# Free order of the four row tiles for matmul chains in a kernel whose order is planned

## The chip, the cores and the metric

The kernel runs on one core of a Trainium2 chip. A core has five engines that work from queues of their own: TensorE (PE), which does matmuls, VectorE (DVE), ScalarE (ACT), GpSimd (POOL), and SyncE (SP), whose queue here only starts DMA transfers. The metric is the device time of one execution in microseconds. In this kernel TensorE is used in three ways: with the whole 128x128 array ("whole" matmuls), as four row tiles of 32 rows that each take matmuls of their own ("row" matmuls, 32x128 in the profile), and as four column tiles of 32 columns (128x32 in the profile, for the weighted values of the attention).

## The reference

A row of x (2048 rows of 448 elements) is layer-normed to xn; then attention and a gated feed-forward both read xn, and their results are added to x. The attention has 16 query heads of 28 elements and one key and one value head. The numbers are float32.

```python
q = (x @ wq).reshape(B, S, H, Dh) ...; k = x @ wk; v = x @ wv
p = softmax(einsum("bhqd,bkd->bhqk", q, k) * Dh ** -0.5)
attention = einsum("bhqk,bkd->bhqd", p, v) ... @ wo
gate, up = xn @ w1, xn @ w3
feed_forward = (silu(gate) * up) @ w2
return x + attention(xn) + feed_forward(xn)
```

## The kernel before

**Precision.** Most matmuls run on operands in a reduced type (fp32r). An operand is split into a high part and the rest, and a product is the sum of high x high, high x rest and rest x high. So each product is a chain of many matmuls that add into one bank of PSUM, of which there are eight.

**Stages.** The 2048 rows are four blocks of 512 columns (`NQ`, `TC`). In the beginning all blocks are normed, transposed (xp) and projected to q, k and v (`project`, line 640: sixteen chains q, four for each block). The weights are loaded, split, used, and written to DRAM split for the later blocks. Then the attention goes in 16 groups of four heads (`NW`): for each head a first score tile gives a bound of the maximum (`leads`, ld), then 15 further score tiles (`product`, line 853, sc, three row matmuls each; head h uses row tile h mod 4), each followed by ScalarE's exponential (line 909). The weighted values (`values`, line 912, av) come in bursts of 6, 6 and 4 key tiles (`BURSTS`); a burst of 6 is 48 matmuls in the profile, one of 4 is 32. Beside the attention the feed-forward goes in 56 steps: gate and up (g, u, `gate_up`, line 754) for 128 hidden columns, and after two or three such steps four down projections (dn, `down`, line 775). The attention's output projection (wo, `out_project`, line 1021) and dn are added to acc, which is stored at the end of a block.

**Chains.** `chain` (line 443) builds q, g, u, dn and wo. With `first=None` it uses whole matmuls (11 for q, g and u). Otherwise every term of 128 rows becomes four row matmuls, one for each row tile: 42 for q, g and u. All matmuls of tile 0 come first, then those of tile 1, 2 and 3; each matmul depends on the one before. A bank may be written by one row tile at a time, so a chain that passes to the next tile waits until its last matmul in the former tile is done: `build` puts a `nop` with a dependency on that matmul in PE's queue. `WHOLE = (3, 2)` says that the first three steps of the feed-forward, and the query projections of the first two blocks, are whole; the last dn and wo are whole as well.

**The planner.** The order of all instructions on all queues is not that of the program text. Every operation is an `Op` with an engine, a modelled cost and latency, a priority (a due time from `due`, `begin` and others plus a correction `PUT` by kind of operation), and the operations it depends on. `Plan.order` (line 173) goes through time and gives each engine that is free its ready operation of the smallest key; for PE each of the four row tiles is a slot that is filled by itself (`SLOTS`). `BOOST` lowers the key of matmuls that continue a product or a chain. An operation is held back if its buffers are short (`MOST`, `SPARE`, `SOON`) or its PSUM bank is read by another engine (`locked`). If PE has nothing for a slot, a second pass takes operations before their time, if `EARLY` buffers are left. `FLIGHT = 4` is the largest number of chains of row matmuls that are begun and not ended: `link` is +1 at the first and -1 at the last matmul of a chain. Several chains may alternate in one tile. The queues of the chip then run in this order, each engine's instructions one after the other; where the model errs, an instruction waits at the head of its queue.

Of the kernel before, what the change touches and what calls it, by code (L numbers as in the profile page):

```python
# [38 lines left out]
ROWS = 4  # L39
BOOST = (97.61, 1.0)  # L40
FLIGHT = 4
WHOLE = (3, 2)
# [8 lines left out]
T0, TG, LEAD, SPAN = 59.41, 51.88, 5.12, 37.1  # L51
XDUE = (18.51, 11.88, 15.8, 24.23)
QDUE, QSTEP = 36.59, 9.52
SINGLE = 2
XSTORE = 13.37, 47.32
MDUE, MRUSH, MSTEP = 35.96, 8, 9.02
MEND = 12.77
# [4 lines left out]
BACKLOG = 1998.39  # L62
LATE = 765.84
HLV = 0
EARLY = 12
BULK = ("w13", "w2", "x", "raw", "raw2", "acc")
SOON = {"acc": 9.76, "h": 11.77, "mb": 12.24, "o": 44.69, "pa": 20.77, "pb": 55.73, "qs": 2, "w13": 109.34,
        "w2": 18.75, "wo": 69.88, "x": 31.37}

PUT = {"ACT ": 25.95, "ACT acc xn": 19.89, "ACT at pa": -2.13, "ACT at pb": 55.24, "ACT at x": -16.88,  # L70
# [3 lines left out]
        "DVE ": -6.21, "DVE acc": 11.86, "DVE acc mi": -6.67, "DVE acc xn": -7.18, "DVE at": 19.67,  # L74
# [8 lines left out]
        "POOL raw": 3.84, "POOL raw w13": -46.77, "POOL raw wo": 4.7, "POOL raw2 w2": 61.66,  # L83
# [12 lines left out]
SPARE = {"acc": 7, "h": 0, "qs": 5, "qt": 1, "raw": 4, "raw2": 1, "w13": 1, "w2": 2, "wo": 1, "x": 1}  # L96
# [23 lines left out]

class Op:
    __slots__ = ("eng", "cost", "lat", "fn", "bufs", "deps", "prio", "n", "wait", "outs", "at", "done", "size", "next", "k", "port", "row", "mode", "prev", "key", "link", "hop", "ins")


class Plan:
# [11 lines left out]
    def op(self, eng, cost, fn, reads=(), writes=(), parts=(), prio=0.0, after=(), lat=None, size=0, also=(), behind=None, k=16, port=False, row=None, mode="a", prev=None, nth=9):  # L137
# [18 lines left out]
        o.prio += PUT.get(eng + " " + " ".join(sorted({b.sort for b in o.bufs})), 0.0)  # L156
        for b in o.bufs:
            b.left += 1
        o.link, o.hop = 0, False
        if prev is not None and prev.row != row:  # L160
            prev.hop = True
        o.key = o.prio - (0.0 if prev is None else BOOST[0] if nth < 3 else BOOST[1])
        o.deps = list(deps.values())
        o.next = []
        for d in o.deps:
            (d.next if eng == d.eng in ("PE", "ACT", "POOL") and not (d is prev and d.row != row) else d.outs).append(o)
        if behind is not None:
            behind.next.append(o)
        o.wait = len(o.deps) + (behind is not None)
        self.ops.append(o)  # L170
        return o

    def order(self):
# [25 lines left out]
        def can(o, early=False):  # L199
# [9 lines left out]
            if early:  # L209
                if any(len(p) - k < EARLY for k, p in zip(need[:2], pools) if k):  # L210
                    return False
            elif any(o.prio > head() + SOON.get(sorts[c], 40.0) for c in cats):
                return False
# [17 lines left out]
        flying = 0  # L231
# [7 lines left out]
        while todo:  # L239
            progress = True  # L240
            while progress:
                progress = False
                for e, row in self.SLOTS:
# [3 lines left out]
                    for o in ready[e]:  # L247
                        if row is not None and (o.row not in (None, row) or o.link > 0 and flying >= FLIGHT):
                            continue
                        if best is not None and (o.key, o.n) >= (best.key, best.n):  # L250
                            continue
                        if e == "SP" and max(queues) - now > BACKLOG and o.prio > 40.0 and o.bufs and any(b.cat in BULK for b in o.bufs):
# [3 lines left out]
                        best = o  # L256
                    if best is None and e == "PE":
                        best = min((o for o in ready[e] if o.row in (None, row) and not (o.link > 0 and flying >= FLIGHT) and
                                    locked(o, now) <= now and can(o, True)),
                                   key=lambda o: (o.key, o.n), default=None)  # L260
# [28 lines left out]
                    if e == "PE":  # L289
# [6 lines left out]
                        flying += o.link  # L296
# [23 lines left out]
            while events and events[0][0] <= now + 1e-6:  # L320
                _, _, kind, o = heapq.heappop(events)
                if kind == "port":
                    continue
# [66 lines left out]
def build(ctx, tc, x, wqkv, w13r, wor, w2, out, flag):  # L390
# [52 lines left out]
    def chain(dst, n, w, width, terms, prio, after=(), whole=True, first=None):  # L443

        o = None
        whole = [d for l, _, r, _, _ in terms for d in l.writers + r.writers] if whole else []
        if first is None:
            todo = [(None, t) for t in terms]
        else:
            todo = [(r, t) for r in [(first + i) % ROWS for i in range(ROWS)] for t in terms if r in t[4]]  # L450
        for i, (r, (lb, lv, rb, rv, _)) in enumerate(todo):
            q = slice(0, P) if r is None else slice(r * RP, (r + 1) * RP)

            def fn(i=i, lb=lb, lv=lv, rb=rb, rv=rv, q=q):
                return nc.tensor.matmul(dst.ap[0:n, 0:width], lv(lb)[q], rv(rb)[q], start=(i == 0),  # L455
                                        stop=(i == len(todo) - 1))
            o = pe(width, fn, reads=[lb, rb], parts=[dst], prio=prio, row=r, prev=o,
                   after=[o] if o is not None else [*after, *whole])
            dst.writers = [o]
            if r is not None:  # L460
                o.link = (i == 0) - (i == len(todo) - 1)
# [605 lines left out]
    for o in todo:  # L1067
# [165 lines left out]
```

## Time and profile before

| | before |
|---|---|
| median of 3 runs | 998.35 us (997.87 to 1003.17) |
| the profiled execution | 1001.47 us |
| its span in the profile | 999.7 us |
| mean granted TensorE clock | 0.994 |
| PE busy | 983.3 us, 98% |
| ACT busy | 644.0 us, 64% |
| DVE busy | 411.8 us, 41% |
| POOL busy | 258.5 us, 26% |
| moved by DMA | 169.10 MB, mean 169 GB/s |

Line 455 is the matmul in `chain`, so all chains have this line and are told apart by the tile that they write (q, g, u, dn, wo); line 860 is that of the scores (sc, ld), 921 that of the values (av). A form such as 32*128 32x448 says 32 active rows, 128 active columns, and a moving operand of 32 rows and 448 columns. Busy time of PE is the time in which at least one matmul runs, and up to four row matmuls run at once; the busy time of a group is counted in the same way, so the groups add up to more than the span.

### The profile page before, as it was taken

Reading aid. Unit: us, or ns where it says so; the run is one execution under the profiler, and the core shown is the slowest. Engines: PE = TensorE matmul, PEld = TensorE weight load, DVE = VectorE, ACT = ScalarE, POOL = GpSimd, SP = SyncE. Lnnn points to the kernel's source line nnn. Section 1 sums busy time; section 2 is a strip of 40 time slices with the busy share of each in tenths; the row PEclk is TensorE's granted clock in tenths of the full one; section 3 lists DMA queues with packets and bytes.
Section 4 is the critical chain, followed back from the end, with each engine's and each line's share of the span. In section 5 each row is a group of like instructions: output and inputs, shape, how many; then the busy total and the mean of one; then the engine's idle time right before and its main releaser. Section 6 shows DMA issues by size and latency. Waiting matters only on the chain.

```text
span 999.7 us, 31015 instructions
## 1 busy us (share of the span) xinstructions
PE 983.3 (98%) x13168; PEld 762.0 (76%) x13168; DVE 411.8 (41%) x956; ACT 644.0 (64%) x1232; POOL 258.5 (26%) x215
## 2 busy tenths in 40 slices
PE   6999999999999999999999999999999999999997
PEld 5778886877778778687786877878877687788675
DVE  7672252534335252525252523544432535252223
ACT  6643476776757667677656767667767676576542
POOL 3233335463304221212122221222122212222201
PEclk9998999999999999999999999999999999999999
DMA  6768677877635344333564345535544353533301
GB/s 239 234 197 296 255 276 269 289 264 268 218 92 184 113 151 141 125 132 125 200 215 132 112 131 171 174 102 176 178 133 152 128 178 114 169 118 144 128 2 40
DMA packets 81769, 169.10 MB, mean 169 GB/s; under 512 B 14940, under 2 KB 41308, under 8 KB 81624
## 3 DMA queue, kind: packets, MB, share of 16 engines
q1 hardware_dynamic: 81624, 167.05, 50.3%
q8 instruction: 105, 1.72, 0.7%
q14 instruction: 40, 0.33, 0.1%
HBM read 124.56 MB, written 40.62 MB: 165 GB/s over the span
## 4 chain that ended last, share of the span: by engine, by line
PE 95%; DMA 2%; DVE 1%; SPq 1%; ACT 0%; POOL 0%; issue 0%; ACTq 0%
PE av L921 22%; PE sc L860 19%; PE u L455 15%; PE g L455 15%; PE dn L455 13%; PE q L455 5%; PE wo L455 4%; PE ld L860 2%; DMA mb<-md 1%; PE xp L612 1%; DMA acc<-x 0%; DMA md<-nm 0%; POOL pa L902 0%; DVE xn L596 0%; SPq L889 0%
## 5 line engine op out<-in xcount | busy, mean ns | idle before, releaser
L909 ACT ACTIVATE pb<-sc 128x512 f32<-128x512 f32 x960 | 514.6, 619 | 181.5 <-PE sc L860 143.5
L860 PE MATMUL sc<-qs,kh 28*128 28x512 f32 (+1 forms) x1920 | 514.3, 403 | 0.3 <-ACT pb L909 0.3
L455 PE MATMUL dn<-w,h 32*128 32x448 f32 (+1 forms) x2400 | 373.3, 367 | 0.0
L455 PEld LDWEIGHTS dn<-w,h 32*128 32x128 f32 (+1 forms) x2400 | 312.8, 184 | 20.0 <-issue 13.8
L860 PE MATMUL sc<-qs,kl 28*128 28x512 f32 x960 | 327.6, 393 | 0.0
L860 PEld LDWEIGHTS sc<-qs,kh 28*128 28x128 f32 (+1 forms) x1920 | 298.1, 184 | 13.8 <-issue 8.5
L921 PE MATMUL av<-pb,vst 128*32 128x512 f32 x1920 | 215.6, 594 | 0.0
L455 PE MATMUL g<-x_0m,w 32*128 32x512 f32 x672 | 180.5, 398 | 0.8 <-ACT pb L909 0.8
L455 PE MATMUL g<-x_2m,w 32*128 32x512 f32 x588 | 180.0, 389 | 0.0
L773 POOL TENSOR_TENSOR h<-t,h 128x512 fp32r<-128x512 f32 x56 | 72.3, 1291 | 410.8 <-DVE h L770 162.4
L455 PE MATMUL u<-x_0m,w 32*128 32x512 f32 x672 | 173.7, 397 | 0.0
L860 PEld LDWEIGHTS sc<-qs,kl 28*128 28x128 f32 x960 | 166.2, 185 | 0.6
L921 PEld LDWEIGHTS av<-pb,vst 128*32 128x32 f32 x1920 | 59.1, 110 | 135.5 <-issue 130.8
L455 PEld LDWEIGHTS g<-x_0m,w 32*128 32x128 f32 x672 | 113.3, 183 | 3.9 <-issue 1.7
L455 PE MATMUL u<-x_6m,w 32*128 32x512 f32 x420 | 115.8, 388 | 0.0
L455 PEld LDWEIGHTS u<-x_0m,w 32*128 32x128 f32 x672 | 110.8, 183 | 4.4 <-issue 3.4
L902 POOL TENSOR_TENSOR pa<-pa,mb 128x512 f32<-128x512 f32 x64 | 82.6, 1297 | 117.6 <-DMA mb<-md 113.6
L455 PE MATMUL g<-x,w 32*128 32x512 f32 (+1 forms) x495 | 111.5, 400 | 0.0
L455 PE MATMUL wo<-wo,oh 32*128 32x448 f32 (+1 forms) x732 | 109.0, 367 | 0.0
L455 PE MATMUL u<-x,w 32*128 32x512 f32 (+1 forms) x495 | 106.6, 394 | 0.0
L455 PEld LDWEIGHTS g<-x_2m,w 32*128 32x128 f32 x588 | 102.9, 183 | 1.6 <-issue 0.8
L455 PE MATMUL g<-x_4m,w 32*128 32x512 f32 x336 | 101.0, 387 | 0.0
(98 smaller groups left out, 1763.6 us busy)
## 6 DMA issues: line engine op xcount, KB each, us to landing
w<-w13s SPq DMA_DIRECT2D x84, 512.0 KB
w<-w2s SPq DMA_DIRECT2D x42, 448.0 KB
mb<-md SPq DMA_DIRECT2D x64, 256.0 KB
w13s<-w SPq DMA_DIRECT2D x28, 512.0 KB
raw<-w SPq DMA_DIRECT2D x28, 256.0 KB
qs<-qd SPq DMA_DIRECT2D x64, 112.0 KB
wo<-wos SPq DMA_DIRECT2D x16, 448.0 KB
w2s<-w SPq DMA_DIRECT2D x14, 448.0 KB
```

What stands on the lines that cost most here:

```text
L455: return nc.tensor.matmul(dst.ap[0:n, 0:width], lv(lb)[q], rv(rb)[q], start=(i == 0), stop=(i == len(todo) - 1))
L612: pe(128, lambda o=o, v=xn[t], t=t, c=c: nc.tensor.transpose(o.ap[:, t * P:(t + 1) * P], v.ap[:, c * P:(c + 1) * P], ident_ap), reads=[ide ...
L773: sub(512, lambda: eng.tensor_sub(hl.ap, t.ap, f32(hh.ap)), reads=[t, hh], writes=[hl], prio=2 * half)
L860: return nc.tensor.matmul(o.ap, kx[v, kt * P:(kt + 1) * P], qx.ap[v], start=(i == 0), stop=(i == 2))
L902: gps(512, lambda: nc.gpsimd.tensor_add(p.ap, p.ap, b.ap), reads=[b], writes=[p], prio=-3.0)
L909: act(512, lambda: nc.scalar.activation(p.ap, o.ap, AF.Exp, scale=SCALE), reads=[o], writes=[p], prio=0.0, after=[sqrt_last])
L921: nc.tensor.matmul(a.ap[32 * i:32 * i + 32], vst_ap[:, kt], p.ap, start=(kt == lo), stop=(kt == hi - 1), skip_group_check=True)
```

## The change

The chain is no longer one sequence over the tiles 0, 1, 2, 3. It becomes four sequences, one for each tile, that belong together as a `Run`. Within a tile the order is as before; between tiles no order is given. The planner begins a sequence (its `head`) in a tile if no other sequence of the same run is at work (`busy`, which ends when the last matmul of the former sequence, its `tail`, is done), if no other chain holds the tile (`held`), and if the run has begun already or fewer than `flight` runs are open. The first matmul of the chain in the planned order clears the bank and the last closes it, and the `nop` before each later head waits for the tail of the sequence before it in the planned order.

The number of open chains is now set by stretches of the plan's time: the table `TILT` has a line for nearly every 10 us from 1 to 950 us, with the limit (3 or 4 up to 70 us, 5 from there, 6 or 7 from 140 to 630, 4 or 5 after that) and corrections of priorities by kind of operation. `WHOLE` becomes (3, 4): the query projections of all four blocks are whole. `EARLY = 56` exceeds the number of pages (38) and pairs (27) of SBUF, so that the second pass takes only operations that need no new one. `BOOST`, `PUT`, `SOON`, `MOST`, `SPARE` and some due times have new values. All instructions other than the q chains and the `nop`s are the same in number and size; their order on every queue is new.

```diff
-BOOST = (97.61, 1.0)
+BOOST = (130.28, 1.02)
+TAKE = 0.0
+TILT = (
+    (1.0, 4, {"PE mi w13 x": -12.26}),
...
+    (200.0, 7, {"ACT at x": 1.76, "ACT at xp": 0.66, "ACT mi t": 10.99, "ACT wq wr": 1.8, "DVE acc xn": 8.8,
+                "PE at pa qs": 7.61, "PE av pb": 0.39, "PE h mi w2 2": -3.51, "PE mi w13 x": -1.43,
+                "POOL wq wr": -6.38, "SP mb": 1.71, "SP w13": 16.06, "SP xt": -2.37}),
...
+    (950.0, 4, {"SP qs": -4.73}),
+)
 FLIGHT = 4
-WHOLE = (3, 2)
+WHOLE = (3, 4)
...
-EARLY = 12
+EARLY = 56
...
-MOST = {"acc": 14, "at": 5, "av": 6, "h": 7, "kv": 2, "lb": 5, "m": 4, "mb": 2, "mi": 7, "mxt": 10, "o": 12,
-        "oh": 8, "pa": 13, "pb": 8, "qp": 6, "qs": 19, "qt": 3, "raw": 12, "raw2": 1, "t": 7, "w13": 21,
-        "w2": 10, "wo": 30, "wq": 14, "wr": 10, "x": 19, "xn": 1, "xp": 16, "xt": 4}
+MOST = {"acc": 12, "at": 5, "av": 4, "h": 9, "kv": 2, "lb": 2, "m": 1, "mb": 2, "mi": 8, "mxt": 2, "o": 13,
+        "oh": 6, "pa": 18, "pb": 8, "qp": 9, "qs": 15, "qt": 3, "raw": 4, "raw2": 1, "t": 13, "w13": 23,
+        "w2": 7, "wo": 26, "wq": 13, "wr": 17, "x": 19, "xn": 1, "xp": 16, "xt": 4}
...
+class Run:
+
+    def __init__(self):
+        self.busy = self.begun = False
+        self.left = 0
+        self.heads = []
+        self.past = None
...
-        o.link, o.hop = 0, False
-        if prev is not None and prev.row != row:
-            prev.hop = True
+        o.run, o.head, o.tail = run, run is not None and prev is None, False
+        if run is not None:
+            run.left += 1
+            if o.head:
+                run.heads.append(o)
...
+        def turn(o):
+
+            return not o.head or not o.run.busy and not held[o.row] and (o.run.begun or flying < flight)
...
-                        if row is not None and (o.row not in (None, row) or o.link > 0 and flying >= FLIGHT):
+                        if row is not None and (o.row not in (None, row) or not turn(o)):
...
+                    run = o.run
+                    if run is not None:
+                        held[row] = not o.tail
+                        if o.head:
+                            run.busy = True
+                            gain = TAKE if run.begun else TAKE + BOOST[1]
+                            flying += not run.begun
+                            run.begun = True
+                            run.heads.remove(o)
+                            for q in run.heads:
+                                q.key -= gain
+                        run.left -= 1
+                        if not run.left:
+                            flying -= 1
+                        elif o.tail:
+                            push(o.done + LOADING, "turn", o)
...
     def chain(dst, n, w, width, terms, prio, after=(), whole=True, first=None):
 
-        o = None
         whole = [d for l, _, r, _, _ in terms for d in l.writers + r.writers] if whole else []
-        if first is None:
-            todo = [(None, t) for t in terms]
-        else:
-            todo = [(r, t) for r in [(first + i) % ROWS for i in range(ROWS)] for t in terms if r in t[4]]
-        for i, (r, (lb, lv, rb, rv, _)) in enumerate(todo):
+        run = None if first is None else Run()
+        ends, count, total = [], [0], sum(1 if first is None else len(t[4]) for t in terms)
+        for r in (None,) if first is None else [(first + i) % ROWS for i in range(ROWS)]:
+            o = None
             q = slice(0, P) if r is None else slice(r * RP, (r + 1) * RP)
...
+            for lb, lv, rb, rv, where in terms:
+                if r is not None and r not in where:
+                    continue
+
+                def fn(lb=lb, lv=lv, rb=rb, rv=rv, q=q):
+                    count[0] += 1
+                    return nc.tensor.matmul(dst.ap[0:n, 0:width], lv(lb)[q], rv(rb)[q], start=(count[0] == 1),
+                                            stop=(count[0] == total))
+                o = pe(width, fn, reads=[lb, rb], parts=[dst], prio=prio, row=r, prev=o, run=run,
+                       after=[o] if o is not None else [*after, *whole])
+                dst.writers = []
+            o.tail = True
+            ends.append(o)
+        dst.writers = ends
         return o
...
-        past = o.prev
-        if past is not None and past.row != o.row:
+        if o.head and o.run.past is not None:
             w = nc.tensor.nop()
-            tc.add_manual_dep(w.ins, past.ins, AFTER, reason="a bank takes one row tile at a time")
+            tc.add_manual_dep(w.ins, o.run.past, AFTER, reason="a bank takes one row tile at a time")
         r = o.fn()
-        if o.hop:
-            o.ins = r.ins.name
+        if o.tail and o.run is not None:
+            o.run.past = r.ins.name
```

More of the change, by code (lines that the diff above doesn't have):

```diff
@@ L61 @@
 AFTER = mybir.DependencyInfo(mybir.DependencyClass.Sync, mybir.DependencyReason.DATA)
[L62 removed]
+BACKLOG = 1911.92
 LATE = 765.84
 HLV = 0
[L65 removed]
+EARLY = 56
 BULK = ("w13", "w2", "x", "raw", "raw2", "acc")
[L67 to L70 removed]
[3 rows of a table removed]
[L74 removed]
[8 rows of a table removed]
[L83 removed]
[3 rows of a table removed]
+SOON = {"acc": 11.67, "h": 18.77, "mb": 12.34, "o": 11.33, "pa": 18.45, "pb": 113.14, "qs": 13.45,
+        "w13": 108.03, "w2": 18.82, "wo": 66.14, "x": 43.13}
+PUT = {"ACT ": 21.91, "ACT acc xn": -2.19, "ACT at pa": -2.13, "ACT at pb": 82.89, "ACT at x": -53.93,
[3 rows of a table added]
+        "DVE ": 4.09, "DVE acc": -3.56, "DVE acc mi": -5.14, "DVE acc xn": -33.05, "DVE at": 7.06,
[8 rows of a table added]
+        "POOL raw": 3.84, "POOL raw w13": -35.46, "POOL raw wo": 9.97, "POOL raw2 w2": 78.84,
[3 rows of a table added]
 PAIRS = 27
@@ L118, in ap @@
         return self.of.ap[:, self.i]
+class Run:
[4 more added lines that the diff above has]
+        self.past = None
 class Op:
-    __slots__ = ("eng", "cost", "lat", "fn", "bufs", "deps", "prio", "n", "wait", "outs", "at", "done", "size", "next", "k", "port", "row", "mode", "prev", "key", "link", "hop", "ins")
+    __slots__ = ("eng", "cost", "lat", "fn", "bufs", "deps", "prio", "n", "wait", "outs", "at", "done", "size", "next", "k", "port", "row", "mode", "prev", "key", "run", "head", "tail", "kind")
 class Plan:
@@ L135, in __init__, with op @@
         self.base = 0.0
-    def op(self, eng, cost, fn, reads=(), writes=(), parts=(), prio=0.0, after=(), lat=None, size=0, also=(), behind=None, k=16, port=False, row=None, mode="a", prev=None, nth=9):
+    def op(self, eng, cost, fn, reads=(), writes=(), parts=(), prio=0.0, after=(), lat=None, size=0, also=(), behind=None, k=16, port=False, row=None, mode="a", prev=None, nth=9, run=None):
         o = Op()
@@ L155, in op @@
         o.bufs = list({id(b): b for b in bufs if b.ap is None}.values())
-        o.prio += PUT.get(eng + " " + " ".join(sorted({b.sort for b in o.bufs})), 0.0)
+        o.kind = eng + " " + " ".join(sorted({b.sort for b in o.bufs}))
+        o.prio += PUT.get(o.kind, 0.0)
+        o.kind += "" if prev is None else " 1" if nth < 3 and o.row is not None else " 2"
         for b in o.bufs:
             b.left += 1
-        o.link, o.hop = 0, False
-        if prev is not None and prev.row != row:
-            prev.hop = True
+        o.run, o.head, o.tail = run, run is not None and prev is None, False
[3 more added lines that the diff above has]
+                run.heads.append(o)
         o.key = o.prio - (0.0 if prev is None else BOOST[0] if nth < 3 else BOOST[1])
@@ L165, in op @@
         for d in o.deps:
-            (d.next if eng == d.eng in ("PE", "ACT", "POOL") and not (d is prev and d.row != row) else d.outs).append(o)
+            (d.next if eng == d.eng in ("PE", "ACT", "POOL") else d.outs).append(o)
         if behind is not None:
@@ L211, in can @@
                     return False
-            elif any(o.prio > head() + SOON.get(sorts[c], 40.0) for c in cats):
+            elif any(o.prio + tilt.get(o.kind, 0.0) > head() + SOON.get(sorts[c], 40.0) for c in cats):
                 return False
@@ L229, in locked @@
             return last
-        flying = 0
+        flying, held, flight, tilt, turns = 0, [False] * ROWS, FLIGHT, {}, list(TILT)
+        def turn(o):
+            return not o.head or not o.run.busy and not held[o.row] and (o.run.begun or flying < flight)
         for o in self.ops:
@@ L239, in order @@
         while todo:
+            while turns and now >= turns[0][0] * 1e3:
+                _, flight, tilt = turns.pop(0)
             progress = True
@@ L247, in order @@
                     for o in ready[e]:
-                        if row is not None and (o.row not in (None, row) or o.link > 0 and flying >= FLIGHT):
+                        if row is not None and (o.row not in (None, row) or not turn(o)):
                             continue
-                        if best is not None and (o.key, o.n) >= (best.key, best.n):
+                        key = o.key + tilt.get(o.kind, 0.0)
+                        if best is not None and (key, o.n) >= (first, best.n):
                             continue
-                        if e == "SP" and max(queues) - now > BACKLOG and o.prio > 40.0 and o.bufs and any(b.cat in BULK for b in o.bufs):
+                        if e == "SP" and max(queues) - now > BACKLOG and o.prio + tilt.get(o.kind, 0.0) > 40.0 and o.bufs and any(b.cat in BULK for b in o.bufs):
                             continue
@@ L255, in order @@
                             continue
-                        best = o
+                        best, first = o, key
                     if best is None and e == "PE":
-                        best = min((o for o in ready[e] if o.row in (None, row) and not (o.link > 0 and flying >= FLIGHT) and
+                        best = min((o for o in ready[e] if o.row in (None, row) and turn(o) and
                                     locked(o, now) <= now and can(o, True)),
-                                   key=lambda o: (o.key, o.n), default=None)
+                                   key=lambda o: (o.key + tilt.get(o.kind, 0.0), o.n), default=None)
                     if best is None:
@@ L295, in order @@
                             lat += INTO[mode]
-                        flying += o.link
                         for r in mine:
@@ L322, in order @@
                 if kind == "port":
+                    continue
+                if kind == "turn":
+                    o.run.busy = False
                     continue
@@ L443, in chain @@
     def chain(dst, n, w, width, terms, prio, after=(), whole=True, first=None):
-        o = None
         whole = [d for l, _, r, _, _ in terms for d in l.writers + r.writers] if whole else []
-        if first is None:
-            todo = [(None, t) for t in terms]
-        else:
-            todo = [(r, t) for r in [(first + i) % ROWS for i in range(ROWS)] for t in terms if r in t[4]]
-        for i, (r, (lb, lv, rb, rv, _)) in enumerate(todo):
-            q = slice(0, P) if r is None else slice(r * RP, (r + 1) * RP)
[L454 to L461, printed above, removed]
+        run = None if first is None else Run()
+        ends, count, total = [], [0], sum(1 if first is None else len(t[4]) for t in terms)
+        for r in (None,) if first is None else [(first + i) % ROWS for i in range(ROWS)]:
+            o = None
+            q = slice(0, P) if r is None else slice(r * RP, (r + 1) * RP)
+            for lb, lv, rb, rv, where in terms:
+                if r is not None and r not in where:
+                    continue
+                def fn(lb=lb, lv=lv, rb=rb, rv=rv, q=q):
[8 more added lines that the diff above has]
+        dst.writers = ends
         return o
```

31 lines of the change are left out of this document (25 added, 6 removed), and 274 rows, old and new, of tables (PUT, TILT).

## The prediction

> **What bounds the kernel now.** I read the summary of the profile first, then the chain of waits, then windows, and only after that single instructions.
>
> ```profile
> span 999.7 us, 31015 instructions
> ...
> PE 983.3 (98%) x13168; PEld 762.0 (76%) x13168; DVE 411.8 (41%) x956; ACT 644.0 (64%) x1232; POOL 258.5 (26%) x215
> ...
> PE 95%; DMA 2%; DVE 1%; SPq 1%; ACT 0%; POOL 0%; issue 0%; ACTq 0%
> ```
>
> TensorE (PE) is busy 98% of the span and is 95% of the chain that ended last; ScalarE, the next engine, works 64%. But "busy" means that at least one matmul runs. In row mode four tiles of 32 rows run side by side, so a busy PE may be a quarter used. The real question is how full the four tiles are. The windows cut the span into its start, two early stretches, the long steady stretch and the end; (x) counts matmuls, PEclk is the granted clock.
>
> ```profile
> 0.00:68.50 68.50, 59.34 (x281) 46.92 (x281) 44.85 (x100) 40.96 (x78) 20.71 (x25) 1.00 0.70 228
> 68.50:95.00 26.50, 26.50 (x143) 20.13 (x145) 12.47 (x32) 6.26 (x11) 11.98 (x10) 0.81 0.78 248
> 95.00:123.22 28.22, 28.22 (x392) 26.61 (x389) 7.66 (x11) 17.30 (x34) 8.83 (x8) 1.00 0.75 281
> 123.22:940.52 817.30, 816.16 (x11872) 631.33 (x11875) 329.94 (x781) 558.64 (x1068) 208.85 (x165) 1.00 0.50 166
> ```
>
> The pitch of a tile: in the timeline of PE four matmuls of 512 columns start every 0.23 us when all tiles are fed (four from 408.64 to 408.75, the next four from 408.86 to 408.97), and one of 448 columns follows its predecessor after 0.204 us (136.68 to 137.29 in three steps).
>
> ```profile
> 408.64 0.38 PE L455 MATMUL g<-x_4m,w 32*128 32x512 f32 x1
> 408.64 0.38 PE L455 MATMUL u<-x_0m,w 32*128 32x512 f32 x1
> 408.74 0.38 PE L455 MATMUL g<-x_0m,w 32*128 32x512 f32 x1
> 408.75 0.38 PE L860 MATMUL sc<-qs,kh 28*128 28x512 f32 x1
> 408.86 0.39 PE L455 MATMUL g<-x_4m,w 32*128 32x512 f32 x1
> 408.87 0.38 PE L455 MATMUL u<-x_2m,w 32*128 32x512 f32 x1
> 408.97 0.39 PE L455 MATMUL g<-x_0m,w 32*128 32x512 f32 x1
> 408.97 0.40 PE L860 MATMUL sc<-qs,kh 29*128 29x512 f32 x1
> ...
> 136.68 0.36 PE L455 MATMUL dn<-w,h 32*128 32x448 f32 x1
> ...
> 137.29 0.36 PE L455 MATMUL dn<-w,h 32*128 32x448 f32 x1
> ```
>
> The work of the steady stretch, 123.22 to 940.52, by groups; the value bursts (av) are in the chain of waits as whole pieces.
>
> ```profile
> L455 PE MATMUL dn<-w,h 32*128 32x448 f32 x2304 | 348.0, 365 | 0.0
> L860 PE MATMUL sc<-qs,kh 29*128 29x512 f32 x903 | 322.3, 414 | 0.3 <-ACT pb L909 0.3
> L921 PE MATMUL av<-pb,vst 128*32 128x512 f32 x1800 | 202.1, 594 | 0.0
> L455 PE MATMUL wo<-wo,oh 32*128 32x448 f32 x672 | 97.8, 367 | 0.0
> L921 PE MATMUL av<-pa,vst 128*32 128x512 f32 x124 | 16.6, 605 | 0.0
> ```
>
> ```profile
> 381.68 3.57 PE av L921 x32
> 400.53 5.29 PE av L921 x48
> ```
>
> Of 11872 matmuls 1924 belong to bursts (four of them to the burst that begins at the window's edge; 45 bursts lie inside, 30 of 48 and 15 of 32), 2304 + 672 = 2976 have 448 columns, and the other 6972 have 512. Filled to the last slot they need 6972 x 0.23 / 4 = 400.9 us and 2976 x 0.204 / 4 = 151.8 us; the bursts take 30 x 5.29 + 15 x 3.57 = 212.3 us. Together that is 765.0 of 817.3 us: **52.3 us of slots stay empty**, 1.16 us for each of the 45 stretches between bursts. PE as a whole stands for only 817.30 - 816.16 = 1.1 us, so the loss is single tiles that run dry beside working ones.
>
> Stretches differ greatly. One of the fullest and one of the emptiest, each with the 448-column group in it:
>
> ```profile
> 385.18:400.46 15.28, 15.28 (x274) 14.88 (x270) 5.43 (x10) 11.41 (x22) 1.17 (x1) 1.00 0.50 154
> 171.72:186.36 14.64, 14.64 (x209) 13.70 (x205) 6.22 (x11) 13.34 (x27) 4.96 (x4) 1.00 0.76 239
> ```
>
> ```profile
> L455 PE MATMUL dn<-w,h 32*128 32x448 f32 x92 | 13.2, 364 | 0.0
> ```
>
> ```profile
> L455 PE MATMUL dn<-w,h 32*128 32x448 f32 x33 | 6.0, 378 | 0.0
> ```
>
> About four of each count are of the burst at the edge, as 274 stands to 270 weight loads. The first holds 270 - 92 = 178 row matmuls of 512 columns and 92 of 448, 10.2 + 4.7 = 14.9 us of slots, so 0.4 us is lost. The second holds 205 - 33 = 172 and 33, 9.9 + 1.7 = 11.6 us of 14.64, so 3.1 us is lost. In both PE is "busy" throughout.
>
> **The change part by part.** *Any free order.* Now a chain (g, u, dn, wo) must take tile 0, then 1, 2, 3, and at most four are open; with tile 2 empty and tile 1 full, a chain that has 1 and 2 to go waits. After the change it takes whichever of its remaining tiles is free, it may begin anywhere, and up to seven are open in the middle of the plan. It adds no matmul: 42 row matmuls per g or u chain as before, and three waits per chain for the bank's earlier tile as before. The price per slot is that of above, so the gain is the empty slots that get filled. Lower bound: zero, if slots are empty because nothing is ready or an in-order wait holds the queue. Upper bound: all 45 stretches like the fullest, 52.3 - 45 x 0.4 = 34 us; the 0.4 is about the change between row mode and burst, which stays. I take about two thirds, **22 us**: nearer the upper end, because the two stretches above carry the same kinds of work and because the whole-PE stop is only 1.1 us, but not all of it, because late semaphores also open short gaps that an order cannot close.
>
> *One chain at a time in a tile.* This takes freedom away: two chains no longer alternate in one tile. Scores still may enter between them. An occupied tile always has its chain's next matmul ready, so with a chain in each tile it costs nothing; with fewer chains the cost is inside the third that I left out.
>
> *First chains whole.* The last four query projections (42 row matmuls each) become 11 full-array matmuls. What they cost now, and the matmuls around them:
>
> ```profile
> 54.81 3.40 PE L455 MATMUL q<-x,wq 128*126 128x512 f32 x14
> ...
> 69.54 3.66 PE L455 MATMUL q<-x,wq 32*126 32x512 f32 x20
> 73.12 1.89 PE L455 MATMUL dn<-w,h 128*128 128x448 f32 x5
> 74.94 5.06 PE L455 MATMUL g<-x,w 32*128 32x512 f32 x11
> 79.93 6.53 PE L455 MATMUL dn<-w,h 128*128 128x448 f32 x22
> ```
>
> ```profile
> 74.00:76.00 2.00, 2.00 (x6) 1.21 (x6) 1.91 (x5) 0.00 (x0) 0.00 (x0) 0.50 0.37 90
> ...
> 78.00:80.00 2.00, 2.00 (x6) 1.05 (x4) 0.00 (x0) 0.00 (x0) 0.00 (x0) 0.50 0.79 251
> ```
>
> A full matmul takes 3.40 / 14 = 0.243 us, so 44 take 10.7 us; 168 row matmuls packed four wide take 168 x 0.23 / 4 = 9.7 us. Packed, the edit would lose 1 us. But from 69.54 twenty of them run alone in one tile for 3.6 us, where their share as whole chains is 20 / 168 x 10.7 = 1.3 us: 2.3 us gained.
>
> *Early stretch.* Right behind, a g chain runs alone for 5 us, 11 matmuls that fill 0.6 us of slots, at half clock. From 68.5 to 95 the clock averages 0.81, which costs 26.5 x 0.19 = 5.0 us. The half clock stands in windows where PE is never idle (2.00 of 2.00) but has one matmul at a time, so here it goes with thin work. If the new order puts anything beside that chain, some of the 5.0 us and of the 4.4 us of empty slots returns; a lone chain, however, can never use two tiles, since its bank takes one at a time. I book half the clock's cost, 2.5 us, so **5 us** for the whole early part with the 2.3. Bounds: -3 (four extra changes of mode, the packed loss of 1 us) to +12 (2.3 + 5.0 + 4.4). The Trainium skill ("TensorE: Matmul & The Clock Gate", Part 1) says that the clock halves after an idle window of about 3.4 us and comes back with sustained work; this trace agrees on two states but halves without an idle PE. By the page a new order with no idle PE would return all 5.0 us, and the time would be 2.5 us lower than forecast.
>
> *Order anew.* All priorities, buffer limits and the table by stretch change the order on every queue, SP's loads and POOL's too, but no DMA is added or removed. DMA is half used in the steady stretch (0.50) and POOL 26% overall, so this moves cover, not bound; in the early stretch (0.78 and 0.75) a late weight load would come out directly, which the -3 covers. At the end:
>
> ```profile
> 978.73 1.45 PE u L455 x7
> 980.17 3.57 PE av L921 x32
> ```
>
> seven u matmuls run nearly alone before the last burst, 7 x 0.23 - 7 x 0.0575 = 1.2 us of empty slots. I book **1 us** (0 to 3).
>
> *Sum.* 22 + 5 + 1 = 28 us: span 999.7 becomes 971.7. The profiled execution took 1001.47 us, 1.8 over its span and 3.1 over the median 998.35; the same 28 us off the median gives **970 us**.
>
> **The rivals.** *Full success.* Every stretch as full as the best and the early bounds: 34 + 12 + 3 = 49 us, 949 us. For it: the best stretch exists. Against: the plan runs on modelled times, and a late semaphore shows in no plan. Chance 0.12.
>
> *Nothing ready.* The tiles run dry for lack of loaded weights, banks or due scores, not of a permitted tile; then only the early 2.3 us remains: 996 us. For it: the emptier stretch has the busier DMA (0.76 against 0.50). Against: DMA is at 0.50 on average and yet 1.16 us per stretch is lost. Chance 0.07.
>
> *The waits take it back.* PE takes its instructions in order, so a wait for a bank's earlier tile stops all four tiles if it is reached too early. There are 106 g and u chains (4452 / 42), and with dn and wo about 206, three waits each: 618. If the denser order reaches each 0.035 us too early, 22 us are lost: 992 us. For it: a matmul lasts 0.38 but its tile is free after 0.23. Against: as many waits are in the order of before and PE stands 1.1 us. Chance 0.08.
>
> *Banks, slower.* Every open chain holds one of eight banks. A score holds a bank for three matmuls, the rest of the last, and its exponential:
>
> ```profile
> L909 ACT ACTIVATE pb<-sc 128x512 f32<-128x512 f32 x960 | 514.6, 619 | 181.5 <-PE sc L860 143.5
> ```
>
> 3 x 0.23 + 0.15 + 0.62 = 1.46 us. Row mode has 817.3 - 212.3 = 605 us for 903 scores, 1.49 per us, so scores need 2.2 banks, and the burst's accumulator one: from five open chains on, scores starve. The change allows seven from 150 to 630 us, some 480 x 605 / 817 = 355 us of row mode. At one bank scores come at 0.68 instead of 1.49 per us, 288 short if it held throughout; if in an eighth, 36 scores trail at ScalarE's 0.62 us, 22 us, and against an otherwise even plan (996) that is 1018 us. For it: the limit rises by three. Against: seven is a limit, not a demand, and scores keep their own priority. Chance 0.13. The Trainium skill ("TensorEngine Tiling (Array Packing)", Gotcha 1) states that row tiles need different banks and raise the pressure on them; the waits per chain agree, the starving no row here shows.
>
> **How the numbers follow.** Forecast 0.60, spread about 955 to 985; success 0.12, nothing ready 0.07, waits 0.08, banks 0.13. The range 944 to 998 takes in the forecast, full success and the two neutral rivals and leaves out the slower one and little beside, about 2 in 10. A measurement tells 0.5% (5 us) from no change. Below 993: 0.60 + 0.12 + 0.08 = 0.80; within: 0.07; slower: 0.13.
>
> **What would show it.** In the profile after: about 0.6 us lost per stretch between bursts in place of 1.16; from 68 to 95 no q with 32 rows and a clock above 0.81; PE still near 98% of the span. Wrong would be: stretches still 1.1 us short (nothing ready), PE standing for more than some 10 us in the steady stretch (waits), or exponentials of ScalarE waiting longer for scores than 143.5 us with bursts that come late (banks).

## The result

The changed kernel takes 970.55 us (median, 969.61 to 971.02) against 1000.76 us of the kernel before in the same comparison; the ratio is 0.9698, 95% interval 0.9662 to 0.9734. The forecast was 970. Whether its steps were right is another matter, and most of what follows is about that.

The summary of the profile after:

```profile
span 968.8 us, 30798 instructions
...
PE 953.3 (98%) x13044; PEld 738.8 (76%) x13044; DVE 408.8 (42%) x956; ACT 640.3 (66%) x1232; POOL 257.5 (27%) x215
...
PE 94%; DMA 3%; ACT 1%; DVE 1%; SPq 1%; issue 0%; ACTq 0%; DVEq 0%
```

The picture is the same, only shorter: PE 98% busy, ScalarE far behind. The 124 matmuls fewer are four query projections (168 row matmuls became 44 whole ones): of the sixteen chains q twelve were whole already, since the first two of every block always are. The windows, with the borders of the kernel before where they mean the same, and from the first burst (110.91) to the first burst of the last group (912.19):

```profile
0.00:68.50 68.50, 59.99 (x277) 46.96 (x278) 43.89 (x102) 41.31 (x78) 21.66 (x26) 1.00 0.71 228
68.50:95.00 26.50, 25.87 (x185) 21.14 (x184) 11.87 (x32) 8.93 (x17) 7.71 (x7) 1.00 0.74 244
95.00:110.91 15.91, 15.91 (x169) 13.02 (x170) 3.19 (x5) 14.51 (x30) 8.57 (x7) 1.00 0.95 315
110.91:912.19 801.28, 801.00 (x11935) 622.50 (x11939) 332.38 (x784) 555.11 (x1069) 211.41 (x167) 1.00 0.54 174
912.19:968.80 56.61, 50.52 (x494) 35.14 (x494) 17.43 (x34) 20.49 (x42) 8.17 (x9) 0.97 0.14 45
```

```profile
L768 PE MATMUL dn<-w,h 32*128 32x448 f32 x2304 | 377.0, 364 | 0.0
...
L768 PE MATMUL wo<-wo,oh 32*128 32x448 f32 x672 | 75.7, 364 | 0.0
```

The steady stretch holds the same 2976 matmuls of 448 columns, the same 45 bursts, and 11935 - 1924 - 2976 = 7035 of 512 columns. So its slots are 404.5 + 151.8 + 212.3 = 768.6 us of 801.3: 32.7 us are empty, 0.73 us per stretch, where it was 52.3 us and 1.16. The span falls by 30.9 us in three parts: the first burst begins 123.22 - 110.91 = 12.3 us earlier; the steady stretch is 817.3 - 801.3 = 16.0 us shorter, although it holds 63 matmuls more (3.6 us, moved out of the early part); and the end is 59.2 - 56.6 = 2.6 us shorter. Put by slots: 19.6 us from fuller tiles in the steady stretch, 12.3 - 3.6 = 8.7 us in the early part, 2.6 us at the end.

The early part, in the timeline of PE after:

```profile
65.81 2.69 PE L768 MATMUL q<-x,wq 128*126 128x512 f32 x11
...
70.08 7.46 PE L768 MATMUL dn<-w,h 128*128 128x448 f32 x36
77.37 2.00 PE L768 MATMUL q<-x,wq 128*126 128x512 f32 x8
...
81.26 0.85 PE L768 MATMUL g<-x,w 32*128 32x512 f32 x3
82.03 2.34 PE L768 MATMUL q<-x,wq 128*126 128x512 f32 x9
```

The longest that a row chain runs alone in this timeline is 0.85 us (three g matmuls at 81.26), where it was 5 us. The 36 whole dn matmuls stand in one piece at full clock, 7.46 us; before, 22 of them took 6.53 us, mostly at half clock. The granted clock from 68.5 to 95 is 1.00 where it was 0.81.

### The profile page after: what moved, and what is told of

It is laid out like the page before. It is cut to its first block, busy times and chain, and to the rows that moved or that the text cites. A ratio compares the mean times of both kernels' runs of the same rounds, so it can differ in the third digit from the quotient of the medians.

```text
span 968.8 us, 30798 instructions
## 1 busy us (share of the span) xinstructions
PE 953.3 (98%) x13044; PEld 738.8 (76%) x13044; DVE 408.8 (42%) x956; ACT 640.3 (66%) x1232; POOL 257.5 (27%) x215
## 4 chain that ended last, share of the span: by engine, by line
PE 94%; DMA 3%; ACT 1%; DVE 1%; SPq 1%; issue 0%; ACTq 0%; DVEq 0%
PE av L1235 23%; PE sc L1174 19%; PE g L768 15%; PE u L768 15%; PE dn L768 13%; PE wo L768 4%; PE q L768 3%; PE ld L1174 1%; DMA qs<-qd 1%; DMA scr<-x 1%; DMA md<-nm 1%; PE xp L926 0%; DMA qd<-qt 0%; ACT pb L1223 0%; DMA acc<-x 0%
## 5 line engine op out<-in xcount | busy, mean ns | idle before, releaser
L1223 ACT ACTIVATE pb<-sc 128x512 f32<-128x512 f32 x960 | 509.7, 619 | 178.4 <-PE sc L1174 148.8
L1174 PE MATMUL sc<-qs,kh 28*128 28x512 f32 (+1 forms) x1920 | 508.9, 401 | 0.6 <-ACT pb L1223 0.6
L768 PE MATMUL dn<-w,h 32*128 32x448 f32 (+1 forms) x2400 | 398.8, 364 | 0.0
L768 PEld LDWEIGHTS dn<-w,h 32*128 32x128 f32 (+1 forms) x2400 | 336.2, 183 | 17.7 <-issue 11.6
L1174 PEld LDWEIGHTS sc<-qs,kh 28*128 28x128 f32 (+1 forms) x1920 | 301.3, 184 | 18.3 <-issue 12.3
L768 PE MATMUL u<-x_0m,w 32*128 32x512 f32 x672 | 181.2, 395 | 0.0
L768 PE MATMUL u<-x_6m,w 32*128 32x512 f32 x420 | 120.6, 388 | 0.0
L768 PEld LDWEIGHTS u<-x_0m,w 32*128 32x128 f32 x672 | 116.2, 183 | 1.4 <-issue 0.8
L768 PE MATMUL g<-x,w 32*128 32x512 f32 (+1 forms) x495 | 104.3, 394 | 0.0
L768 PE MATMUL u<-x_2m,w 32*128 32x512 f32 x336 | 103.6, 390 | 0.0
L768 PE MATMUL u<-x_4m,w 32*128 32x512 f32 x336 | 102.3, 388 | 0.0
```

Of the source, the lines that this page charges most:

```text
L1174: return nc.tensor.matmul(o.ap, kx[v, kt * P:(kt + 1) * P], qx.ap[v], start=(i == 0), stop=(i == 2))
L1223: act(512, lambda: nc.scalar.activation(p.ap, o.ap, AF.Exp, scale=SCALE), reads=[o], writes=[p], prio=0.0, after=[sqrt_last])
```

## The experiments

A number that compares all kernels is used below: the empty slots between the first burst and the first burst of the last group. In each kernel that window holds nearly the same work: 4900 matmuls belong to bursts or have 448 columns and take 364.1 us, and each of the others has 512 columns and takes 0.0575 us of slots (0.23 / 4). The rest of the window is called empty. It gives 52.3 us for before and 32.7 for after. This number is a time, so stretches at half clock inside the window count as empty as well; there are none in before and after, but the other orders have up to 7 us of them, and the table at the end of this section lists them. Theory F says that the *permission* to take any free tile fills the slots; theory O that the *particular order* does, which the many numbers of the plan select.

**A nudged order of before.** Every correction of `PUT` is moved by a random amount of about 1 us (standard deviation).

```diff
-PUT = {"ACT ": 25.95, "ACT acc xn": 19.89, "ACT at pa": -2.13, "ACT at pb": 55.24, "ACT at x": -16.88,
+PUT = {"ACT ": 26.89, "ACT acc xn": 18.49, "ACT at pa": -2.81, "ACT at pb": 55.61, "ACT at x": -17.90,
...
```

> The kernel before, with every correction in PUT moved by a random amount of about 1 us (normal, standard deviation 1.0). Nothing else changes: tiles in the order 0 to 3, at most four open chains, no table by stretch. Theory F (the permission to take any free tile fills the empty slots; the numbers behind the order matter little) expects the time of before within 1%: 990 to 1010 us, and about 52 us of empty slots in the 45 stretches between bursts. Theory O (the particular order fills them, found by trying many; any other order of the same rules is emptier) expects 1015 to 1035 us, with 65 us or more of empty slots.

1043.02 us, ratio 1.0437 (1.0397 to 1.0476).

```profile
134.72:976.27 841.55, 839.83 (x11918) 647.93 (x11918) 327.25 (x775) 561.04 (x1069) 213.29 (x169) 0.99 0.49 159
```

73.9 us empty, as theory O expects; the time is above the ranges of both theories. The same rules with slightly other priorities are 43 us slower: the kernel before owed its time to the particular order it had. Part of the 43 us is the clock. Before and just after the first burst this order has long pieces at half clock:

```profile
60.00:134.72 74.72, 74.02 (x540) 61.20 (x538) 29.53 (x66) 31.30 (x59) 22.86 (x19) 0.87 0.72 250
134.72:164.72 30.00, 28.61 (x227) 18.44 (x230) 5.75 (x19) 17.31 (x33) 11.54 (x10) 0.76 0.59 214
```

They cost about 74.72 x 0.13 = 9.7 us and 30 x 0.24 = 7.2 us, where before lost 5.0 us ahead of its first burst and none in the steady stretch. Without its 7.2 us the steady stretch has 66.7 us empty.

**Free order alone.** The changed code with all numbers of before:

```diff
-BOOST = (130.28, 1.02)
+BOOST = (97.61, 1.0)
 TAKE = 0.0
-TILT = (
...
-)
+TILT = ()
...
-WHOLE = (3, 4)
+WHOLE = (3, 2)
...
-EARLY = 56
+EARLY = 12
```

> The new chain and planner code (any free tile, one chain at a time in a tile) with all numbers of the kernel before: at most four open chains, no table by stretch, old PUT, MOST, EARLY, query projections of the last two blocks in rows. Theory F expects most of the gain: 975 to 985 us and 30 to 40 us of empty slots in the steady stretch (before 52, after 33). Theory O expects no gain over before, 1000 to 1025 us, and 50 us or more empty.

1017.58 us, ratio 1.0178 (1.0141 to 1.0216): slower than before.

```profile
112.68:947.82 835.14, 833.04 (x11822) 643.59 (x11821) 327.81 (x781) 553.62 (x1063) 209.95 (x166) 1.00 0.50 163
```

73.0 us empty, no better than the nudged order of before. Theory F is refuted here for the free tile; the limit of open chains is still four in this run, and the next run has that part of the permission too. Only the early part is better: the first burst begins at 112.68, against 134.72 in the nudged order.

**A nudged order of after.** The same kind of nudge as in the first run, on the kernel after; all rules and the table stay.

> The kernel after, with every correction in PUT moved by a random amount of about 1 us, as in the nudged kernel before; the table by stretch, the free order and whole query projections stay. Theory F expects 965 to 985 us, close to after, and about 33 us of empty slots. Theory O expects the gain to be gone: 1000 to 1025 us with 50 us or more empty, although every rule of the change is still in place.

1017.12 us, ratio 1.0160 (1.0121 to 1.0198).

```profile
121.02:957.75 836.73, 836.61 (x11946) 648.90 (x11945) 329.86 (x778) 552.58 (x1067) 212.86 (x169) 1.00 0.51 165
```

67.5 us empty. Every rule of the change is in place, the limits of up to seven open chains too, and the whole gain is gone, 47 us. So the rules do not suffice. The execution with the profile was the longest of the four (1023.2 us; the others 1014.29 to 1017.28) and lost some 6.4 us to half clock ahead of the first burst and 2.2 us behind it; without the latter 65.3 us are empty, still twice what after has.

**Query projections in rows.**

```diff
-WHOLE = (3, 4)
+WHOLE = (3, 2)
```

> The kernel after with WHOLE = (3, 2): the last four query projections in rows again. By the prediction's step the early part alone loses some 2 to 5 us: 973 to 976 us, the later stretches as in after. Theory O expects more, since a changed early part shifts everything that the table by stretch was made for: 990 to 1015 us, of which the early part takes no more than 10 and the rest are empty slots in the 45 stretches.

1013.67 us, ratio 1.0137 (1.0098 to 1.0177).

```profile
116.46:948.90 832.44, 831.13 (x11817) 638.53 (x11816) 328.63 (x783) 551.54 (x1064) 209.62 (x166) 1.00 0.51 164
```

The early part takes 5.6 us longer (116.46 against 110.91), within what was expected; but the steady stretch has 70.6 us empty. The last of these projections starts at 101.36 us in its timeline,

```profile
101.36 0.39 PE L768 MATMUL q<-x,wq 32*126 32x512 f32 x1
```

so the 37.9 us (70.6 - 32.7, of which 3.4 are half clock) lost after the first burst are not the edit's own work: the order that the table was made for is gone. A single constant cannot be undone alone in a planned kernel, and what the whole projections are worth by themselves stays open.

**Two waits.** Each `nop` before a new tile is written twice in the program; the order of all other instructions is that of after.

```diff
-            w = nc.tensor.nop()
-            tc.add_manual_dep(w.ins, o.run.past, AFTER, reason="a bank takes one row tile at a time")
+            for _ in range(2):
+                w = nc.tensor.nop()
+                tc.add_manual_dep(w.ins, o.run.past, AFTER, reason="a bank takes one row tile at a time")
```

> The kernel after in its own order, with every wait of PE for a bank's earlier row tile doubled: 618 more waits in PE's queue, all already fulfilled when reached. If an instruction of this kind costs all four tiles time at the head of the queue (the rival of the waits: 0.035 us each), 985 to 995 us. If it is hidden behind the matmuls that run, 969 to 973 us.

969.93 us, ratio 0.9677 (0.9639 to 0.9716), as after.

```profile
110.82:913.15 802.33, 801.75 (x11932) 622.31 (x11932) 331.58 (x784) 555.04 (x1069) 211.47 (x167) 1.00 0.55 174
```

33.9 us empty against 32.7. But as far as the traces show, the edit added nothing. Both executions have 30798 instructions, as many on every engine in the one as in the other, and of the some 618 waits only two stand there as instructions of their own with the line of the `nop`, in either run and at the same times:

```profile
L1387 PEldq EVENT_SEMAPHORE  x2: 51/51/51, 110.3 to 170.0; - x2
```

```profile
L1388 PEldq EVENT_SEMAPHORE  x2: 51/51/51, 110.3 to 170.0; - x2
```

(the first in after, the second in this run). The other waits have no record of their own, and no second wait has one. So this run does not show what a wait costs. What it does give is the repeatability of the comparison: the same order once more, 0.6 us from after in time and 1.2 us in empty slots.

**More nudged orders.** One more of before, and one of the free order with the numbers of before; one time each.

> The kernel before with another random nudge of PUT (standard deviation 1.0). Theory S (the rules of the change and the found order both count, and free order is worth 20 to 30 us between orders of equal standing) expects 1025 to 1045 us, as the first nudge gave 1043, with 70 us or more empty in the steady stretch. Theory O (the found order alone counts, and the first nudge was unlucky) expects 1010 to 1022 us, like the free orders.

1033.18 us.

```profile
131.44:969.58 838.14, 838.12 (x11838) 650.41 (x11838) 329.85 (x779) 556.04 (x1065) 208.33 (x164) 0.99 0.50 160
```

> Free order with the numbers of before (as in the run of free order alone, four open chains, no table), PUT nudged by the same kind of random amounts. Theory S expects 1005 to 1022 us, 15 us or more under the nudged orders of before; theory O expects the same spread as these, 1015 to 1045 us.

1017.21 us.

```profile
109.77:947.00 837.23, 835.06 (x11852) 646.37 (x11851) 330.96 (x780) 551.83 (x1064) 211.34 (x167) 1.00 0.51 166
```

By their times both agree with theory S, free orders some 16 to 26 us under those of before, although 1017 lies in the range of theory O too. But the windows say where: empty slots are 75.1 and 73.4, nearly the same; the first burst begins at 131.44 and 109.77. Half clock hides no difference: behind the first burst it costs 30 x 0.20 = 6.0 us in the one and 30 x 0.11 = 3.3 us in the other,

```profile
131.44:161.44 30.00, 30.00 (x286) 20.37 (x289) 12.17 (x35) 16.39 (x31) 10.48 (x9) 0.80 0.66 223
```

```profile
109.77:139.77 30.00, 28.73 (x280) 17.29 (x283) 1.38 (x2) 15.81 (x32) 8.59 (x7) 0.89 0.99 360
```

which leaves 69.1 and 70.1. So between orders of equal standing the new rules gain in the early part, not in the steady stretch, where the prediction had put it.

**Without the rule of one chain in a tile.** Free order alone, and once more with nudged numbers, one time each:

```diff
-            return not o.head or not o.run.busy and not held[o.row] and (o.run.begun or flying < flight)
+            return not o.head or not o.run.busy and True and (o.run.begun or flying < flight)
```

> Free order alone with the numbers of before, but without the rule of one chain at a time in a tile: several chains may alternate in one tile, as before the change. By the prediction's step the rule costs nothing or little, so leaving it out gives 1005 to 1020 us (1017 with it). If the rule carries the gain of the free order, 1030 to 1050 us.

1036.44 us.

```profile
116.65:968.28 851.63, 850.73 (x11846) 660.65 (x11845) 326.44 (x782) 558.64 (x1064) 210.35 (x167) 1.00 0.49 161
```

> Free order without the rule of one chain in a tile, numbers of before, PUT nudged with the same random amounts as in the nudged free order (1017 with the rule). If the rule, not the free choice of the tile, is what separates the orders that were not searched, this gives 1028 to 1045 us, as the first run without it (1036). If that run was only an unlucky order, 1010 to 1024 us.

1036.30 us.

```profile
111.71:965.52 853.81, 851.91 (x11867) 661.99 (x11866) 331.24 (x783) 558.27 (x1069) 212.98 (x168) 1.00 0.49 160
```

88.1 and 89.1 us empty, against 73.0 and 73.4 with the rule. Free choice of the tile without the rule is *worse* in the steady stretch than the fixed order (73.9 and 75.1; without half clock the distance is larger, 86 to 87 against 67 to 69): the rule is needed to make up for it.

**The rule with a fixed order.** As free order alone, but a chain's next tile must be the next number; one time:

```diff
-            return not o.head or not o.run.busy and not held[o.row] and (o.run.begun or flying < flight)
+            return not o.head or o is o.run.heads[0] and not o.run.busy and not held[o.row] and (o.run.begun or flying < flight)
```

> Tiles in the order 0 to 3 and numbers of before, but one chain at a time in a tile, no table. If the rule of one chain in a tile is what saves 15 to 20 us between free order with it (1017) and without it (1036), by itself, this gives 1010 to 1022 us. If the rule helps only where a chain may choose its tile, it gives 1028 to 1048 us, like the nudged orders of before.

1019.87 us.

```profile
120.64:944.23 823.59, 822.81 (x11716) 637.03 (x11715) 327.59 (x775) 553.12 (x1062) 206.85 (x163) 1.00 0.50 163
```

67.6 us empty, the first burst at 120.64. One chain at a time in a tile, with the tiles still in the order 0 to 3, gives nearly all that free order with the rule gives (1017); 3 us tells nothing where two orders of one kind can be 10 us apart (1043 and 1033). Among orders that were not searched, the rule is worth 19 us by time in the free order and 13 to 23 us in the fixed one, but in different places. In the free order it is the steady stretch (73 against 88 to 89 us empty). In the fixed order the first burst comes 11 to 14 us earlier, and behind it there is 4 to 5 us less half clock; without the half clock the steady stretch is 65.3 us empty against 66.7 and 69.1, hardly a difference. And the free choice filled no slots in any of these orders: with the rule 70.1 to 71.3 us are empty against 65.3 in the fixed order, without it 86 to 87 against 67 to 69. These are one or two orders a cell.

**The same search for both.** Both rules, from the numbers of before, each with a table by stretch found with the same effort (the first lines are those of the fixed order).

```diff
-TILT = ()
+TILT = (
+    (1.0, 4, {'DVE xt': 1.16, 'PE at pb qs': -6.19}),
+    (10.0, 4, {'DVE xt': 1.16, 'PE at pb qs': -6.19, 'PE av pa pb': 27.36}),
...
+)
```

> The rules of before (tiles in the order 0 to 3, chains may alternate in a tile, query projections of two blocks in rows, all numbers of before), with a table by stretch of its own: for each 10 us of the plan the best of 120 random changes of corrections and of the limit of open chains was kept. Theory O (the found order fills the slots) expects that the same search helps the fixed order too: 980 to 996 us, 45 us or less empty in the steady stretch. Theory R (the free order is what makes a fuller order possible) expects no gain over before: 998 to 1010 us, 50 us or more empty.

994.05 us, ratio 0.9937 (0.9913 to 0.9961).

```profile
118.35:929.89 811.54, 811.54 (x11863) 627.93 (x11862) 329.40 (x782) 560.16 (x1068) 209.73 (x166) 1.00 0.52 170
```

> The free order with one chain at a time in a tile, all other numbers of before, and a table by stretch found with the same effort and the same random numbers as for the fixed order. Theory O expects it within 10 us of the fixed order with its table: 980 to 998 us. Theory R expects it 15 us or more faster than that: 970 to 985 us against 998 or more.

997.18 us, ratio 0.9972 (0.9950 to 0.9994).

```profile
112.15:932.74 820.59, 819.73 (x11807) 629.49 (x11807) 327.18 (x780) 552.68 (x1063) 209.24 (x165) 1.00 0.52 167
```

47.1 us empty in the fixed order with its table, fewer than before's 52.3; 59.3 in the free order, down from 73. The search pays in both, and the fixed order ends 3 us ahead, with intervals that overlap. By time both fall in the ranges of theory O; 47.1 is a little above the 45 that it expected. Theory R, that the free order is what makes a fuller order possible, finds no support. It is not refuted either, because the two did not start level. The numbers of before were fitted to the fixed order (as the nudges show, which cost 33 to 43 us) and start there at 1000 us; in the free order they are an unfitted start, at 1017.6. The same search gained 6 us in the one and 20 in the other. The kernel after has a much fuller order than either (32.7). Whether a longer search would bring the fixed order there too, or whether the free order wins only then, was not tried and stays open.

| order | rules | time, us | empty in the steady stretch, us | of it half clock, us | first burst, us |
|---|---|---|---|---|---|
| as it was | before | 1000.8 | 52.3 | 0 | 123.2 |
| nudged | before | 1043.0, 1033.2 | 73.9, 75.1 | 7.2, 6.0 | 134.7, 131.4 |
| not searched | fixed, one chain in a tile | 1019.9 | 67.6 | 2.3 | 120.6 |
| not searched, nudged | free, one chain in a tile | 1017.6, 1017.2 | 73.0, 73.4 | 1.7, 3.3 | 112.7, 109.8 |
| not searched, nudged | free, chains alternate | 1036.4, 1036.3 | 88.1, 89.1 | 1.7, 1.7 | 116.7, 111.7 |
| nudged | after | 1017.1 | 67.5 | 2.2 | 121.0 |
| own table | before | 994.1 | 47.1 | 0 | 118.4 |
| own table | free, one chain in a tile | 997.2 | 59.3 | 3.4 | 112.2 |
| as it is | after | 970.6 | 32.7 | 0 | 110.9 |

The column of half clock is the length of a window times what its granted clock falls short of 1, as above.

## Why the prediction was right, and where it was not

The time was right: 970 forecast, 970.55 measured, a gain of 28 forecast and 30.9 in the profile. The reading of the bottleneck was right too: empty slots of single tiles, not whole-PE stops, were the reserve, and their filling is most of the gain (19.6 of 30.9 us).

*The steady stretch* was forecast at 22 us, "two thirds" of 34; measured 19.6. The size is right, the cause is not, so the hit is luck. The step said that a chain "takes whichever of its remaining tiles is free", "so the gain is the empty slots that get filled". Free order alone left 73.0 us empty, and the whole set of rules with nudged numbers 67.5. What filled the slots is the order that the table and the other numbers select, under these rules: nudge the numbers and the gain is gone. The prediction filed this under "order anew" and, but for 1 us at the end, priced it at nothing ("this moves cover, not bound"). That was the failed step: the new rules without a found order gain none of the 20 us. Whether the fixed order could reach 32.7 us with an order found by a longer search stays open. The best stretch that it took as the reachable level existed under the fixed rules, which was already a sign that the rules did not forbid it.

*One chain at a time in a tile* was booked as taking freedom away at no cost or a small one. It did the opposite: without it the free order has 15 us more empty, while in the fixed order it changes the steady stretch by a few us at most. Why was not shown.

*The early part* was forecast at 5 us (bounds -3 to 12); measured 8.7 by slots. The 2.5 us of clock were mis-sized: the half clock is gone altogether, 5.0 us. The rest, 3.7, is near the 2.3 for the query projections, but was not separated from the new order.

*The end* was forecast at 1 us (0 to 3); measured 2.6.

*The rivals.* "Nothing ready" is out, as after has 0.73 us lost per stretch (forecast 0.6). Waits that stop all of PE are out by the prediction's own sign: PE stands for 801.28 - 801.00 = 0.3 us in the steady stretch, not for more than 10. Whether a wait that comes too early leaves single tiles empty was not tested; it would be a part of the 32.7 us. Banks: exponentials wait for scores about as before,

```profile
L1223 ACT ACTIVATE pb<-sc 128x512 f32<-128x512 f32 x960 | 509.7, 619 | 178.4 <-PE sc L1174 148.8
```

148.8 us against 143.5, and the same 45 bursts lie in a stretch that is 16 us shorter; nothing shows that the allowance of seven open chains starved the scores. A rival that was missing is the one that nearly all experiments met: the same rules with an order that was not searched, slower by 13 to 17 us than before.

## What to carry to other kernels

In a kernel whose order is planned, a change of the rules and the search that follows it must be told apart: nudge the numbers of both sides and compare orders of equal standing before crediting the rule. One constant changed under a plan that was fitted stretch by stretch (`WHOLE`) cost 43 us here, most of it in stretches where the constant does not act, so an ablation is read from the stretch in which it acts, not from the total. Before an ablation is read at all, look in its trace for what the edit was to add: the doubled waits stand in the program, and the trace has none of them. And where an engine is "98% busy", count slots: the reserve of 52 us was visible in no busy share. Empty slots and half clock look alike in such a count, so read the granted clock beside it.

## What the runs showed of the hardware

The granted clock halves without an idle PE. In the nudged order of before, windows before and in one such half-clock piece:

```profile
118.30:121.80 3.50, 3.50 (x39) 3.19 (x35) 0.00 (x0) 1.50 (x3) 0.98 (x1) 1.00 0.59 232
121.80:125.30 3.50, 3.50 (x28) 3.14 (x25) 0.69 (x1) 0.90 (x2) 0.00 (x0) 1.00 0.23 76
125.30:128.70 3.40, 3.40 (x18) 2.61 (x15) 0.00 (x0) 0.00 (x0) 0.00 (x0) 0.50 1.01 372
128.70:132.10 3.40, 3.40 (x11) 2.62 (x9) 2.66 (x5) 0.86 (x2) 0.00 (x0) 0.50 0.79 297
```

PE is busy in every one of these microseconds. Four full row tiles would start 3.5 / 0.23 x 4 = 61 matmuls in such a window; after one with 28, less than half, the clock is 0.50. The second nudged order, free order alone and its nudged order, each up to the first burst:

```profile
60.00:131.44 71.44, 71.38 (x594) 61.39 (x592) 23.68 (x52) 28.34 (x53) 23.71 (x19) 0.87 0.73 246
```

```profile
60.00:112.68 52.68, 51.34 (x571) 45.57 (x569) 21.34 (x51) 28.60 (x54) 19.95 (x17) 1.00 0.84 284
```

```profile
60.00:109.77 49.77, 49.57 (x532) 42.69 (x531) 21.60 (x47) 25.64 (x51) 19.16 (x17) 1.00 0.80 266
```

About 0.13 x 74.72 = 9.7 and 0.13 x 71.44 = 9.3 us of the some 20 us by which free orders begin their first burst earlier thus go with the clock. The Trainium skill ("TensorE: Matmul & The Clock Gate", Part 1) names idle windows of about 3.4 us as what halves the clock; in the piece above, and in the one that the prediction shows, stretches of about that length with one or two of four row tiles at work went before it, and an idle PE did not. That thin work causes it was seen in these rows and not tested by a run of its own. The order of the instructions does not settle it alone: the kernel before had a mean clock of 0.999 in an execution of 996.04 us and of 0.991 in one of 1003.36 us.
